# Two feed-forwards in split single precision: whole products in the first, seven block products kept for the second

## The chip, the core and the metric

The kernel runs on one core of a Trainium2 chip. The metric is device time in microseconds, as the median of several runs. TensorE (PE) does the matmuls, VectorE (DVE), ScalarE (ACT) and GpSimd (POOL) the element-wise work, SyncE (SP) issues the loads and stores.

## What is computed

Two batches of eight heads of attention over 768 positions: each query sees the keys within 16 positions and 24 block summaries (the maximum of 32 keys, the mean of 32 values). The result, 1,536 tokens of 512 numbers, goes through two feed-forwards.

```python
def _moe_ref(x, w_in, w_out):
    h = x @ w_in                      # 512 -> 2048
    g = h * np.cos(h)
    return (g @ w_out).astype(np.float32)

def _moe2_ref(x, w_in, w_out):
    h = x @ w_in
    relu6 = np.clip(h + 3.0, 0.0, 6.0)
    g = h * relu6 / 6.0
    return (g @ w_out).astype(np.float32)
```

The weights arrive in 64-bit floats.

## The kernel before

**Precision.** Every operand of a feed-forward matmul is split into a rounded part and its remainder (`whi`/`wlo`, `xhi`/`xlo`, `ghi`/`glo`), and a product is three matmuls: hi x hi, lo x hi, hi x lo.

**Steps.** The tokens are three blocks of 512 (`blk`), the hidden width is 16 slices of 128 (`f`) for each feed-forward (`m`). `plan` lists steps (m, blk, f, c0, c1) in groups of four slices; the blocks' direction turns with each group. A step is an input product (`mm1` or half of an `mm1_set`), the nonlinearity (`middle`, L796) and an output product (`mm2`, L853: 12 matmuls summed over the group's four slices in four banks of PSUM, then added to `total` by `close`, L893). The first 16 steps (`NEARLY`) work on halves of 256 tokens, as soon as the attention has delivered them; the next four are plain.

**Plain product** (`mm1`, L764): 12 matmuls of 512 columns into one bank; `middle` reads h from PSUM.

**Seven block products** (`mm1_set`, L708). From step `SETS` = 20 on, two slices of one block go together. The two slices and the two halves of the contraction form a 2 x 2 scheme: seven products of 256 columns, six matmuls each, instead of eight. That needs seven combined weight blocks for each pair of slices (`convert_pair`, L411, into `phi`/`plo`; two pairs are held), combined token blocks (`tees`, L673; `first_tees`, L702, rebuilds the first feed-forward's input as a sum first), and for every set two copies and five adds on 256 columns from PSUM into `hs` (L744 and the helper L389). `middle` then reads h from `hs`.

**Weights.** `nearest` (L431) loads a 64-bit slice into one of two `raw` buffers and rounds it to single precision in one of two pairs `cv_y`, `cv_t`: two conversions, a shift (L462), a merge (L464), an add (L466). `split` (L403) makes the rounded part (the helper `copy`, L389) and the remainder (L406). `convert` (L394) does this for a plain slice: six slots for output slices, four for input slices, which lie in the `phi` tiles.

**Nonlinearity.** In the first feed-forward: a rounding on ScalarE (L819), a subtraction (L821), the sine (L823), h times it (L825), then the rounded part (L389) and the remainder (L834). Three buffers for `c` (`ch_c`), four for `g`.

**Order.** All of this is recorded as operations with dependencies by keys. `Graph.run` gives each a due time and places them, with modelled costs, on the engines that may do them; the result is a fixed instruction order for each engine. Where the planner sees a gap before a matmul, `fill` (L839) puts matmuls on zeros (L844, L849) there. The output product of step s is recorded `LAG` = 2 steps behind its input product.

Of the kernel before, what the change touches and what calls it, by code (L numbers as in the profile page):

```python
# [11 lines left out]
F32 = mybir.dt.float32  # L12
# [17 lines left out]
LAG = 2  # L30
# [158 lines left out]
def attention_two_ffn(  # L189
# [47 lines left out]
    NPLAIN = GROUPS[0][0]  # L237
    SETS = NEARLY + NPLAIN

# [23 lines left out]
    def ring(p, name, n, shape, dtype=F32):  # L263
# [8 lines left out]
    per = -(-NPLAIN // NPAIR)  # L272
# [121 lines left out]
    def convert(n, side):  # L394
# [3 lines left out]
        i = slot(*slices[n]) if side == "out" else n  # L398
        y, _, yk, _ = nearest(n, side)
        new = ["room"] if NW0 <= n < NW1 else []  # L400
# [8 lines left out]
    def convert_pair(p):  # L409
# [250 lines left out]

    tx, hs = {"hi": [], "lo": []}, []
    NH = 4
    PAUSE = 0.3
# [7 lines left out]
    def tees(b, buf, bk):  # L671
# [29 lines left out]

    def first_tees(b):  # L702

        for kk in range(NK):
            G.op({"POOL": pool(TOK), "DVE": dve(TOK)}, lambda e, kk=kk: VEC[e].tensor_tensor(
                total[NBLK - 1][:, kk, :], xhi[b][:, kk, :].bitcast(F32), xlo[b][:, kk, :].bitcast(F32), ALU.add),
                r=["room"] + [(n, b, kk, o) for n in ("xh", "xl") for o in range(UPB)],
                w=[("total", NBLK - 1, kk)], twice=True)  # L708
        tees(b, lambda: total[NBLK - 1], ("total", NBLK - 1))
# [78 lines left out]
    def ring_of(s):  # L788

        if s < NEARLY:  # L790
            return s % NC, s % NG

        return s % NC1, (3, 1, 0, 2)[(s - NEARLY) % NG1]

    def middle(s):
        N = plan[s][4] - plan[s][3]  # L796
        i, n = ring_of(s)
        ck, gk = ("c", i), ("gh", n)
        room = ["room"] if i >= NC or n >= NG else []
# [11 lines left out]
        def c():  # L811
            return ch_c[i][:, 0:N]

        def gh():
            return ghi[n][:, 0:N]

        if plan[s][0] == 0:

            G.op({"ACT": act(N) + 0.05}, lambda e: nc.scalar.activation(  # L819
                c().bitcast(I32), h(), AF.Identity, bias=quarter, scale=0.5 / math.pi), r=hk + room, w=[ck])  # L820
# [247 lines left out]
```

## Time and profile before

| | us |
|---|---|
| median of 3 runs (614.90 to 615.78) | 615.45 |
| profiled execution, its own time | 615.68 |
| its span, first to last instruction | 614.0 |
| TensorE busy | 592.5 |
| VectorE busy | 515.4 |
| ScalarE busy | 389.2 |
| GpSimd busy | 230.4 |

Busy time is the sum over instructions, idle time is what lies between them. A line such as "idle before, releaser" says what ended the idle time. The granted clock is a share of 2.4 GHz.

### The profile page before, as it was taken

How to read it: one execution, taken by the hardware profiler on the slowest of the kernel's cores; microseconds unless marked ns; L12 is line 12 of the kernel's file. 1: busy time of each engine (PE TensorE's matmuls, PEld its weight loads, DVE VectorE, ACT ScalarE, POOL GpSimd, SP SyncE). 2: the span in 40 equal slices, each digit the busy share in tenths (PEclk: the TensorE clock that was granted, in tenths of full speed). 3: DMA queues.
4: the chain of work that ended last, by engine and by line, in shares of the span. 5: the costliest groups of instructions: out<-in, count | busy, mean ns of one | idle time of the engine just before them, and what ended most of it. 6: DMA issues, size and time to landing. Idle time of an engine off the chain costs nothing.

```text
span 614.0 us, 11095 instructions
## 1 busy us (share of the span) xinstructions
PE 592.5 (97%) x4244; PEld 519.5 (85%) x4244; DVE 515.4 (84%) x916; ACT 389.2 (63%) x828; POOL 230.4 (38%) x216
## 2 busy tenths in 40 slices
PE   9989899998998999999989999999999999999997
PEld 6678698887897888988978888999898989889895
DVE  4889997699999999899999999989869984984644
ACT  4889997675667667657776675685845643462321
POOL 5245531444232743473455554434334311520110
PEclk9999999999999999999999999999999999999999
DMA  8768631012112222111212012122312320200111
GB/s 275 226 233 254 183 122 52 2 69 69 34 36 69 69 69 69 70 68 70 76 62 70 25 46 69 49 90 98 108 69 70 114 92 1 70 1 1 69 70 68
DMA packets 17141, 51.57 MB, mean 84 GB/s; under 512 B 2112, under 2 KB 2112, under 8 KB 17088
## 3 DMA queue, kind: packets, MB, share of 16 engines
q1 hardware_dynamic: 17088, 50.86, 25.2%
q8 instruction: 33, 0.54, 0.4%
q14 instruction: 20, 0.16, 0.1%
HBM read 47.71 MB, written 3.15 MB: 83 GB/s over the span
## 4 chain that ended last, share of the span: by engine, by line
PE 55%; DVE 17%; ACT 6%; issue 3%; POOL 2%; DVEq 0%; ACTq 0%; POOLq 0%
PE bank_a L874 15%; PE bank_d L731 12%; PE bank_b L874 7%; PE bank_c L874 7%; PE bank_e L731 6%; PE bank_c L731 6%; DVE ch_c L821 2%; DVE hs L744 2%; DVE glo L834 1%; DVE ch_c L825 1%; DVE cv_t L464 1%; DVE ch_c L830 1%; ACT ch_c L823 1%; POOL cv_y L466 1%; ACT ch_c L819 1%
## 5 line engine op out<-in xcount | busy, mean ns | idle before, releaser
L466 POOL TENSOR_TENSOR cv_y<-cv_t,cv_y 128x512 int32<-128x512 int32 x29 | 42.4, 1463 | 75.9 <-DVE cv_t L464 64.8
L744 DVE TENSOR_TENSOR hs<-bank_d,hs 128x256 f32<-128x256 f32 x108 | 45.1, 421 | 29.3 <-PE bank_d L731 27.2
L834 POOL TENSOR_TENSOR glo<-ch_c,ghi 128x512 fp32r<-128x512 f32 (+1 forms) x28 | 34.2, 1227 | 52.5 <-ACT ghi L389 47.2
L389 ACT CAST ghi<-ch_c 128x512 fp32r<-128x512 f32 (+1 forms) x74 | 43.5, 592 | 11.6 <-DVE ch_c L825 5.4
L828 ACT ACTIVATE ch_c<-hs,three 128x512 f32<-128x512 f32 x48 | 33.7, 722 | 26.8 <-DVE hs L744 26.3
L464 DVE SCALAR_TENSOR_TENSOR cv_t<-raw,cv_t 128x512 int32<-128x512 int32 x64 | 49.2, 780 | 0.2
L457 ACT ACTIVATE cv_t<-raw 128x512 f32<-128x512 f32 x59 | 39.3, 670 | 6.2 <-DMA raw<-in_w_out_dram 2.3
L823 ACT ACTIVATE ch_c<-ch_c,half_pi 128x512 f32<-128x512 f32 (+1 forms) x56 | 35.8, 659 | 8.4 <-DVE ch_c L821 8.3
L830 DVE SCALAR_TENSOR_TENSOR ch_c<-ch_c,hs 128x512 f32<-128x512 f32 x48 | 36.9, 778 | 4.1 <-ACT ch_c L828 2.6
L447 ACT ACTIVATE cv_y<-raw 128x512 int32<-128x512 uint32 x54 | 35.8, 671 | 4.4 <-DVE wlj_out L406 3.5
L834 DVE TENSOR_TENSOR glo<-ch_c,ghi 128x512 fp32r<-128x512 f32 (+1 forms) x54 | 37.0, 692 | 1.7 <-POOL ghi L389 0.7
L731 PE MATMUL bank_d<-xhi,phi 128*128 128x256 f32 x170 | 34.7, 286 | 3.3 <-DVE hs L744 2.4
L731 PEld LDWEIGHTS bank_d<-xhi,phi 128*128 128x128 f32 x170 | 28.4, 189 | 8.3 <-DVE hs L744 3.9
L834 POOL TENSOR_TENSOR glj<-ch_c,ghj 128x512 fp32r<-128x512 f32 x11 | 15.9, 1443 | 51.5 <-ACT ghj L389 48.4
L462 DVE TENSOR_SCALAR cv_t<-cv_t 128x512 int32<-128x512 int32 x64 | 32.5, 516 | 2.3 <-ACT cv_t L457 2.2
L731 PE MATMUL bank_d<-xlo,phi 128*128 128x256 f32 x170 | 34.2, 283 | 0.0
L406 POOL TENSOR_TENSOR plo<-cv_y,phi 128x512 fp32r<-128x512 f32 (+1 forms) x16 | 18.6, 1161 | 41.6 <-DVE phi L389 33.8
L731 PE MATMUL bank_d<-xhi,plo 128*128 128x256 f32 x170 | 34.2, 282 | 0.0
L819 ACT ACTIVATE ch_c<-hs,quarter 128x512 int32<-128x512 f32 x36 | 24.9, 720 | 13.2 <-DVE hs L744 13.1
L821 DVE SCALAR_TENSOR_TENSOR ch_c<-hs,ch_c 128x512 f32<-128x512 f32 x36 | 31.2, 889 | 0.8 <-ACT ch_c L819 0.5
L825 POOL TENSOR_TENSOR ch_c<-hs,ch_c 128x512 f32<-128x512 f32 x14 | 20.7, 1486 | 29.5 <-ACT ch_c L823 29.5
L389 ACT COPY hs<-bank_d 128x256 f32<-128x256 f32 x39 | 14.5, 372 | 26.9 <-PE bank_d L731 26.5
(359 smaller groups left out, 2023.5 us busy)
## 6 DMA issues: line engine op xcount, KB each, us to landing
raw<-in_w_in_dram SPq DMA_DIRECT2D x32, 512.0 KB, 3.5
raw<-in_w_out_dram SPq DMA_DIRECT2D x32, 512.0 KB, 3.4
vcat<-in_vw_dram SPq DMA_DIRECT2D x12, 384.0 KB, 4.3
ktile<-in_kt_dram SPq DMA_DIRECT2D x8, 384.0 KB, 4.4
qt<-in_q_dram SPq DMA_DIRECT2D x12, 256.0 KB, 5.4
total<-in_vw_dram SPq DMA_DIRECT2D x16, 128.0 KB, 3.9
out_dram<-total SPq DMA_DIRECT2D x8, 256.0 KB, 2.0
vnat<-in_vw_dram SPq DMA_DIRECT2D x8, 128.0 KB, 5.8
```

The costliest lines, as they stand in the source:

```text
L389: nc.scalar.copy(o, i) if e == "ACT" else VEC[e].tensor_copy(o, i)
L447: nc.scalar.activation(y, low.bitcast(U32), AF.Copy, scale=2.0 ** -29)
L457: nc.scalar.activation(o, a, AF.Copy, scale=2.0 ** -112)
L464: G.op({"DVE": dve(DM)}, lambda e: nc.vector.scalar_tensor_tensor(t, high, -0x80000000, t, ALU.bitwise_and, ALU.bitwise_or), r=[rk], w=[tk ...
L466: G.op({"POOL": pool(DM), "DVE": dve(DM)}, lambda e: VEC[e].tensor_tensor(y, t, y, ALU.add), r=[tk], w=[yk], twice=True)
L731: nc.tensor.matmul(o, wt[i][:, A[a], kk * P:(kk + 1) * P], xt[:, kk, :], start=first and n + kk == 0, stop=n + kk == 3, skip_group_check=True)
L744: G.op({"DVE": dve(HALF)}, lambda e: nc.vector.tensor_tensor(o[0](), a, b[0](), ALU.add), r=[ak, b[1], "room"], w=[o[1]])
L821: G.op({"DVE": dve(N)}, lambda e: nc.vector.scalar_tensor_tensor(c(), h(), 0.5 / math.pi, c().bitcast(I32), ALU.mult, ALU.subtract), r=hk, ...
L823: G.op({"ACT": act(N) + 0.1}, lambda e: nc.scalar.activation(c(), c(), AF.Sin, bias=half_pi, scale=2.0 * math.pi), w=[ck], table="sin")
L830: G.op({"DVE": dve(N)}, lambda e: nc.vector.scalar_tensor_tensor(c(), c(), 6.0, h(), ALU.min, ALU.mult), r=hk, w=[ck], twice=bool(both))
L834: G.op({"DVE": dve(N), "POOL": pool(N)}, lambda e: VEC[e].tensor_tensor(glo[n][:, 0:N], c(), gh().bitcast(F32), ALU.subtract), r=[ck, gk], ...
L874: nc.tensor.matmul(acc(s, i)[0], l, r, start=first, stop=end and p == 2 and (N == TOK or i % 2 == 1), skip_group_check=N < TOK)
```

## The change

The first feed-forward takes plain products for all its steps: `SETS` becomes the first step of the second feed-forward (56), and `first_tees` goes. The `phi` tiles hold six input slices then (`PER` = 3 in each of two), as many as the output slots; a freed slot takes the slice six ahead. Pairs are formed for the second feed-forward alone: the first two when the last reader of the three slots in their tile is done. Between step 16 and `SETS`, `c` and `g` have five buffers each: two `hs` buffers serve as `c`, and one token block of the `tees` of block 0, not yet needed, as `g` (`LENT`). There the output product follows three steps behind (`LAG1`). The order of first products, nonlinearities and output products is written as a list `events`, from which `assign` gives each step its `g` buffer.

```diff
-LAG = 2
+LAG, LAG1 = 2, 3
...
-    NPLAIN = GROUPS[0][0]
-    SETS = NEARLY + NPLAIN
+    SETS = next(s for s in range(NSTEP) if plan[s][0])
...
-    NW0, NW1 = NPLAIN, 6
+    NW0, NW1 = 4, 6
     NPAIR = 2
+    PER = 3
...
-        t[f // per][:, f % per * 2:f % per * 2 + 2, :].rearrange("p a c -> p (a c)") for f in range(NPLAIN)]}
+        t[f // PER][:, f % PER * 2:f % PER * 2 + 2, :].rearrange("p a c -> p (a c)") for f in range(PER * NPAIR)]}
...
-    NC, NC1 = 3, 3
+    NC, NCL = 3, 5
     ch_c = ring(main, "ch_c", NC, [P, TOK])
-    NG, NG1 = LAG + 1, 4
+    NG, NG1, NGL = 3, 4, 5
...
-        i = slot(*slices[n]) if side == "out" else n
+        i = slot(*slices[n]) if side == "out" else n % (PER * NPAIR)
...
-            also = [(n, "in", f) for n in ("whi", "wlo") for f in range(NPLAIN) if f // per == i] if p < per + NPAIR else []
+            also = [(n, "in", PER * i + f) for n in ("whi", "wlo") for f in range(PER)] if p < NF // 2 + NPAIR else []
...
+    LENT = (0, 0)
...
+                if (b, t) == LENT:
+                    hk, lk = hk + [("gh", NG1)], lk + [("gl", NG1)]
...
-    def first_tees(b):
...
-    def ring_of(s):
-
-        if s < NEARLY:
-            return s % NC, s % NG
-
-        return s % NC1, (3, 1, 0, 2)[(s - NEARLY) % NG1]
+    gslot = {}
+
+    def assign():
...
+    def gbuf(part, n):
+        if n == NG1:
+            return tx[part][LENT[0]][:, LENT[1]].rearrange("p a c -> p (a c)")
+        return {"hi": ghi, "lo": glo}[part][n]
+
+    def cbuf(s):
+
+        i = s % (NCL if NEARLY <= s < SETS else NC)
+        return (ch_c[i], ("c", i)) if i < NC else (hs[i - NC], None)
...
-    for n in range(NW0):
+    for n in range(PER * NPAIR):
         for side in SIDES:
             convert(n, side)
-    for n in range(NW0, NW1):
-        convert(n, "out")
...
     pending = []
     for s in range(NSTEP):
+        if s < SETS:
+            events += [("first", s), ("middle", s)]
+        elif (s - SETS) % 2 == 0:
+            while len(pending) > 2:
+                events.append(("second", pending.pop(0)))
+            events += [("set", s), ("middle", s), ("middle", s + 1)]
+        events.append(("used", s))
+        pending.append(s)
+        lag = LAG if s < NEARLY else (LAG1 if s < SETS else 2)
+        while pending and pending[0] <= s - lag and (s < SETS or (s - SETS) % 2):
+            events.append(("second", pending.pop(0)))
+    events += [("second", r) for r in pending]
+    assign()
...
-        if s == SETS:
-            for c in dict.fromkeys(x[1] for x in plan[s:s + NPLAIN * NBLK]):
-                first_tees(c)
...
+        elif s == uses[m, f]:
+            now = s
+            if n < NF - PER * NPAIR:
+                convert(n + PER * NPAIR, "in")
+            elif n < NF:
+
+                gone.add(n % (PER * NPAIR))
+                for i in range(NPAIR):
+                    if gone >= set(range(PER * i, PER * i + PER)):
+                        gone -= set(range(PER * i, PER * i + PER))
+                        convert_pair(NF // 2 + i)
+            elif n % 2:
+                convert_pair(n // 2 + NPAIR)
```

What it moves stands in the engines' lists. The first place is TensorE behind the four plain steps of block 2, where slices 4 and 5 begin. In the lists L731 is the set's line before and L726 after, L775 the plain product's line after, L874 and L896 the output product's. Before, the first set:

```order
L731 MATMUL bank_d0_107<-xhi2_96,phi0_69 128x256 x2
L731 MATMUL bank_d0_107<-xhi2_96,plo0_71 128x256 x2
L731 MATMUL bank_d0_107<-xlo2_99,phi0_69 128x256 x2
L731 MATMUL bank_d1_108<-txhi2_1611,phi0_69 128x256 x2
L731 MATMUL bank_d1_108<-txhi2_1611,plo0_71 128x256 x2
L731 MATMUL bank_d1_108<-txlo2_1614,phi0_69 128x256 x2
```

After, at the same place: the product of slice 3, the last of the four, then the output product of slice 0, and inside its end the product of slice 4, which is plain now:

```order
L775 MATMUL bank_c1_106<-xhi2_96,phi1_70 128x512 x4
L775 MATMUL bank_c1_106<-xhi2_96,plo1_72 128x512 x4
L775 MATMUL bank_c1_106<-xlo2_99,phi1_70 128x512 x4
L896 MATMUL bank_a0_102<-txhi0_1665,whi_out0_73 128x512
L896 MATMUL bank_a0_102<-txhi0_1665,wlo_out0_77 128x512
L896 MATMUL bank_a0_102<-txlo0_1668,whi_out0_73 128x512
...
L775 MATMUL bank_d0_107<-xhi2_96,phi1_70 128x512 x2
L896 MATMUL bank_c0_105<-txhi0_1665,whi_out0_73 128x512
```

Slice 4's products of 256 columns became products of 512 that need neither the token blocks `tx` nor adds; `txhi0` here is the lent buffer with g in it.

The second place is ScalarE in the last attention units, with the exponentials of the softmax (L600, after L599), the sine (L823, after L845) and the first feed-forward's rounding (L819, after L841). Before:

```order
L600 ACT_TABLE_LOAD
L600 ACTIVATE es_122,sm_132<-bank_c_105,nmx_130 128x120 x4
L600 ACTIVATE es_122,sm_132<-bank_c_106,nmx_130 128x120 x4
L389 COPY total_100<-bank_a_103 128x2x256
L819 ACTIVATE ch_c_85<-bank_d_108,quarter 128x256
L389 COPY pts_126<-bank_b 120x512
L819 ACTIVATE ch_c_86<-bank_d_107,quarter 128x256
L600 ACTIVATE es_123,sm_131<-bank_c_105,nmx_129 128x120 x4
L600 ACTIVATE es_123,sm_131<-bank_c_106,nmx_129 128x120 x4
L389 CAST xhi_96<-bank_e 128x4x128
L823 ACT_TABLE_LOAD
```

After:

```order
L599 ACT_TABLE_LOAD
L599 ACTIVATE es_122,sm_132<-bank_c_105,nmx_130 128x120 x4
L599 ACTIVATE es_122,sm_132<-bank_c_106,nmx_130 128x120 x4
L841 ACTIVATE ch_c_86<-bank_d_107,quarter 128x256
L845 ACT_TABLE_LOAD
L845 ACTIVATE ch_c_85<-ch_c_85,half_pi 128x256
L845 ACTIVATE ch_c_86<-ch_c_86,half_pi 128x256
L446 ACTIVATE cv_y_81<-raw_67 128x512
L388 COPY pts_126<-bank_b 120x512
L388 CAST ghi_88<-ch_c_85 128x256
L599 ACT_TABLE_LOAD
L599 ACTIVATE es_123,sm_131<-bank_c_105,nmx_129 128x120 x4
```

Two softmaxes (units in `es_122` and `es_123`) that shared one table now have the sine between them: two table loads more in the whole list, 16 where there were 14.

The third place is TensorE at the handover from the first feed-forward to the second, in the list of the change: the last reads of `phi0` as a plain slice, and the first set on pair 8 in the same tile.

```order
L775 MATMUL bank_e_109<-xhi0_94,phi0_69 128x512 x2
L775 MATMUL bank_e_109<-xhi0_94,plo0_71 128x512 x4
L775 MATMUL bank_e_109<-xlo0_97,phi0_69 128x512 x4
L896 MATMUL bank_a0_102<-txhi0_1665,whi_out3_76 128x512
...
L896 MATMUL bank_c0_105<-glo1_92,whi_out1_74 128x512
L726 MATMUL bank_d0_107<-xhi2_96,phi0_69 128x256 x2
L726 MATMUL bank_d0_107<-xhi2_96,plo0_71 128x256 x2
L726 MATMUL bank_d0_107<-xlo2_99,phi0_69 128x256 x2
L726 MATMUL bank_d1_108<-txhi2_1667,phi0_69 128x256 x2
```

Between the last read and the first set stand 48 matmuls of 512 columns, 36 of output products and 12 of slice 15. Before, a whole set of pair 7 (42 of 256) and 46 of output products stood there.

## Rows read from the trace of the kernel before

**Rows 1.** The page, busy us, share of the span and instructions.

```profile
PE 592.5 (97%) x4244; PEld 519.5 (85%) x4244; DVE 515.4 (84%) x916; ACT 389.2 (63%) x828; POOL 230.4 (38%) x216
```

**Rows 2.** Stretches: us, PE, PEld, DVE, ACT, POOL busy, granted clock, DMA, GB/s.

```profile
124.00:144.12 20.12, 19.85 (x101) 16.77 (x100) 18.99 (x32) 15.05 (x29) 6.39 (x7) 1.00 0.19 68
144.00:154.00 10.00, 8.15 (x52) 7.30 (x51) 9.88 (x16) 4.58 (x9) 5.81 (x4) 0.88 0.32 91
144.12:360.78 216.66, 208.78 (x1283) 186.22 (x1282) 203.19 (x348) 145.45 (x265) 99.60 (x73) 0.99 0.19 62
360.78:609.60 248.82, 246.85 (x1520) 220.81 (x1518) 194.85 (x349) 128.63 (x234) 74.52 (x60) 1.00 0.18 61
```

**Rows 3.** The same from 144.12 us, for L731, L874 and L849 alone.

```profile
144.12:360.78 216.66, 107.37 (x822) 104.01 (x821) 0.99 0.19 62
144.12:360.78 216.66, 111.75 (x457) 84.29 (x457) 0.99 0.19 62
144.12:360.78 216.66, 1.42 (x4) 0.69 (x4) 0.99 0.19 62
```

**Rows 4.** TensorE's waits, 144 to 361 us: us in total, times, longest.

```profile
PE bank_d L731 <- DVE hs L744: 4.3, 5, 1.9
PE bank_e L731 <- DVE hs L744: 2.2, 4, 1.0
PE bank_d L731 <- ACT hs L389: 0.7, 1, 0.7
```

**Rows 5.** Timeline of TensorE, 354 to 361 us: start, us, instruction.

```profile
354.28 0.39 PE L874 MATMUL bank_a<-ghi,whi_out 128*128 128x512 f32 x1
...
357.91 0.40 PE L731 MATMUL bank_d<-xhi,phi 128*128 128x256 f32 x2
...
360.54 0.40 PE L731 MATMUL bank_d<-xlo,phi 128*128 128x256 f32 x2
360.78 0.40 PE L874 MATMUL bank_a<-whj_out,ghj 128*128 128x512 f32 x1
```

**Rows 6.** The same, a plain product, 129 to 132 us.

```profile
129.03 1.09 PE L780 MATMUL bank_d<-xhi,phi 128*128 128x512 f32 x4
...
131.78 0.28 PE L874 MATMUL bank_a<-ghi,whi_out 128*128 128x256 f32 x1
```

**Rows 7.** The same, 148 to 154 us.

```profile
148.41 0.40 PE L874 MATMUL bank_c<-ghi,whi_out 128*128 128x512 f32 x1
150.66 0.51 PE L731 MATMUL bank_d<-xhi,phi 128*128 128x256 f32 x2 [1.85 <-DVE hs L744]
...
153.53 0.63 PE L874 MATMUL bank_b<-ghi,wlo_out 128*128 128x512 f32 x1
153.96 0.63 PE L874 MATMUL bank_c<-ghi,wlo_out 128*128 128x512 f32 x1
```

**Rows 8.** The page's groups: count, busy us, mean ns, idle before.

```profile
L466 POOL TENSOR_TENSOR cv_y<-cv_t,cv_y 128x512 int32<-128x512 int32 x29 | 42.4, 1463 | 75.9 <-DVE cv_t L464 64.8
L744 DVE TENSOR_TENSOR hs<-bank_d,hs 128x256 f32<-128x256 f32 x108 | 45.1, 421 | 29.3 <-PE bank_d L731 27.2
L464 DVE SCALAR_TENSOR_TENSOR cv_t<-raw,cv_t 128x512 int32<-128x512 int32 x64 | 49.2, 780 | 0.2
L462 DVE TENSOR_SCALAR cv_t<-cv_t 128x512 int32<-128x512 int32 x64 | 32.5, 516 | 2.3 <-ACT cv_t L457 2.2
L406 DVE TENSOR_TENSOR plo<-cv_t,phi 128x512 fp32r<-128x512 f32 x23 | 16.8, 729 | 2.1 <-ACT phi L389 1.9
```

**Rows 9.** Timeline of ScalarE, 111 to 113 us.

```profile
111.56 1.28 ACT L823 ACT_TABLE_LOAD   x1
112.86 0.91 ACT L823 ACTIVATE ch_c<-ch_c,half_pi 128x256 f32<-128x256 f32 x2
```

**Rows 10.** Timeline of TensorE, 379 us.

```profile
379.03 0.74 PE L874 MATMUL bank_a<-whi_out,glo 128*128 128x512 f32 x2 [1.26 <-DVE glo L834]
```

**Rows 11.** TensorE's waits, 84 to 124 us.

```profile
PE bank_d L780 <- DVE ch_c L825: 1.3, 2, 0.9
```

More of the change, by code (lines that the diff above doesn't have):

```diff
@@ L397, in convert @@
             return
-        i = slot(*slices[n]) if side == "out" else n
+        i = slot(*slices[n]) if side == "out" else n % (PER * NPAIR)
         y, _, yk, _ = nearest(n, side)
-        new = ["room"] if NW0 <= n < NW1 else []
+        new = ["room"] if NW0 <= n < NW1 and side == "out" else []
         split(lambda: whi[side][i], lambda: wlo[side][i], y.bitcast(F32), [yk] + new, ("whi", side, i), ("wlo", side, i), DM)
@@ L700, in tees @@
         parts(0, b22, down)
-    def first_tees(b):
[L704 to L709, printed above, removed]
     def mm1_set(s, due):
@@ L786, in mm1 @@
                 ], w=[hk], due=due + (2 * p + k0 // 2) * 2 * mm(n))
-    def ring_of(s):
-        if s < NEARLY:
-            return s % NC, s % NG
-        return s % NC1, (3, 1, 0, 2)[(s - NEARLY) % NG1]
+    gslot = {}
+    def assign():
+        free, kept = list(range(NG)), []
+        for what, s in events:
+            if what == "second":
+                kept.append(gslot[s])
+            elif what == "middle":
+                n = NG if s < NEARLY else (NGL if s < SETS else NG1)
+                free += kept
+                kept = []
+                for k in range(n):
+                    if k not in free and k not in [gslot[r] for r in gslot if r not in done]:
+                        free.insert(0, k)
+                gslot[s] = next(k for k in free if k < n)
+                free.remove(gslot[s])
+            if what == "second":
+                done.add(s)
+    done, events = set(), []
+    def gbuf(part, n):
[5 more added lines that the diff above has]
+        return (ch_c[i], ("c", i)) if i < NC else (hs[i - NC], None)
     def middle(s):
         N = plan[s][4] - plan[s][3]
-        i, n = ring_of(s)
-        ck, gk = ("c", i), ("gh", n)
-        room = ["room"] if i >= NC or n >= NG else []
+        n = gslot[s]
+        late_c = NEARLY <= s < SETS and s % NCL >= NC
+        ck = [("h", s % NCL - NC, t) for t in range(2)] if late_c else [cbuf(s)[1]]
+        gk = ("gh", n)
+        room = ["room"] if late_c or n >= NG else []
         if s < SETS:
@@ L856, in mm2 @@
         begin, end = opens[s], closes[s]
-        wi, n = slot(m, f), ring_of(s)[1]
-        parts = (("whi", whi, "gh", ghi), ("wlo", wlo, "gh", ghi), ("whi", whi, "gl", glo))
+        wi, n = slot(m, f), gslot[s]
+        parts = (("whi", whi, "gh", "hi"), ("wlo", wlo, "gh", "hi"), ("whi", whi, "gl", "lo"))
         order = [[(p, i) for i in (i0, i0 + 1)] for p in range(3) for i0 in (0, 2)]
@@ L866, in go @@
                 for p, i in group:
-                    l, r = parts[p][1]["out"][wi], parts[p][3][n][:, 0:N]
+                    l, r = parts[p][1]["out"][wi], gbuf(parts[p][3], n)[:, 0:N]
                     if m == 0:
@@ L967, in switch @@
         wlo["out"] += ring(pool, "wlj_out", NW1 - NW0, [P, DM], F32R)
-        ch_c.extend(ring(pool, "ch_d", NC1 - NC, [P, TOK]))
         ghi.extend(ring(pool, "ghj", NG1 - NG, [P, TOK], F32R))
@@ L990, in second @@
             convert(slices.index((m, f)) + NW1, "out")
+    gone = set()
     pending = []
     for s in range(NSTEP):
+        if s < SETS:
[11 more added lines that the diff above has]
+    assign()
+    now = 0
+    for what, s in events:
         m, b, f, _, _ = plan[s]
         n = slices.index((m, f))
-        if s == SETS:
-            for c in dict.fromkeys(x[1] for x in plan[s:s + NPLAIN * NBLK]):
-                first_tees(c)
-        if s < SETS:
+        if what == "first":
+            now = s
             mm1(s, when(s))
+        elif what == "set":
+            now = s
+            mm1_set(s, when(s))
+        elif what == "middle":
             middle(s)
-        elif (s - SETS) % 2 == 0:
-            mm1_set(s, when(s))
-            middle(s)
-            middle(s + 1)
-        if s == uses[m, f] and n % 2:
-            convert_pair((n + 1) // 2 - 1 + NPAIR)
-        pending.append(s)
-        while pending and pending[0] <= s - LAG and (s < SETS or (s - SETS) % 2):
-            second(pending.pop(0), when(s) + 2.6)
-    for r in pending:
-        second(r, when(NSTEP) + 2.6)
+        elif what == "second":
+            second(s, when(now) + 2.6)
+        elif s == uses[m, f]:
+            now = s
+            if n < NF - PER * NPAIR:
[8 more added lines that the diff above has]
+                convert_pair(n // 2 + NPAIR)
+        else:
+            now = s
     with tc.manual_schedule():
```

21 lines of the change are left out of this document (10 added, 11 removed).

## The prediction

> **What bounds the kernel now.** I read the page first: TensorE is busy for 592.5 of 614.0 us and VectorE for 515.4 [rows 1]. So close to full, the question is not which engine bounds but how much of TensorE's time is neither work nor needed. The stretches answer it. From 144.12 us, where the first seven-product set starts, to 360.78 us, where the second feed-forward's first output product starts, lie 216.66 us, in which VectorE is busy for 203.19, that is 94% [rows 2]. In the same stretch stand 822 matmuls of 256 columns (L731), 456 of 512 (L874; the 457th starts at its end) and 4 filler matmuls of 512 columns on zeros (L849) [rows 3].
>
> What they need undisturbed comes from the timeline: 24 matmuls of 256 columns from 357.91 to 360.78 us, 0.1196 us each, and 16 of 512 columns from 354.28 to 357.91, 0.2269 us each [rows 5]. So 822 x 0.1196 + 456 x 0.2269 = 98.3 + 103.5 = 201.8 us of work in 216.66 us: **14.9 us are lost**, 0.9 of it in fillers. The list of TensorE's waits says to whom: nearly all stand before a product (L731) and end with a VectorE add into hs (L744), the longest 1.9 us [rows 4]. After that one the clock falls as well: TensorE starts again at 150.66, the matmuls from 153.53 on come 0.43 us apart instead of 0.227 [rows 7], and the mean granted clock of 144 to 154 us is 0.88 [rows 2], which is the 1.2 GHz level for a part of it. The last stretch, from 360.78 to 609.60, takes 248.82 us for 942 and 576 matmuls, which need 243.4: 5.4 us lost, with VectorE at 78% [rows 2]. VectorE is late where it is fullest, and there TensorE waits.
>
> **The change, part by part.** (1) *Whole products.* 18 sets of 42 matmuls of 256 columns (5.02 us) become 36 steps of 12 matmuls of 512 (24 per pair, 5.45 us): 0.42 us more per pair, 7.6 us in all. The plain steps of the kernel before show 12 of 512 columns in 2.75 us, 0.229 each [rows 6], which gives 8.6. I take 7.8, nearer to the 16 in a row, since most matmuls will stand in such rows. The output products are the same number on both sides.
>
> The Trainium skill ("TensorE: Matmul & The Clock Gate", section on the back-to-back issue gap) gives 262 cycles for 256 columns and 518 for 512, by which two narrow matmuls cost hardly more than a wide one. By its figures the cost would be 10.7 us and the sum 2.9 us higher, an estimate from that page. The trace differs: 0.1196 and 0.2269 us are 287 and 545 cycles at 2.4 GHz, so I give that sum 1 in 100, inside the case "within" below.
>
> (2) *What VectorE and ScalarE lose.* 18 sets x 5 adds of 0.42 us [rows 8] are 38 us off VectorE; the 36 copies of a product into hs, mostly ScalarE's, go with them, and so do the first set of block sums and differences (first_tees and its tees) and the half-slice sums of six pairs. On VectorE's list of the change I count 253 rows from the first 512-wide step to the first add of the second feed-forward; at some 0.56 us each (0.6 for 512 columns, 0.34 for 256) they are about 142 us in some 215, 66% where it was 94%. c and gh now read the product from PSUM, but in five buffers and three steps behind, so a late VectorE no longer stops the next product.
>
> (3) *The 14.9 us.* With the adds gone their waits go, and the fillers: the change's list has no filler behind the attention. What can come back is bounded by zero and by the only plain steps of before, 124.00 to 144.12 us, where TensorE is idle for 0.27 in 20 us [rows 2], 2.7 us over 197. I take 1.0, because that stretch still had VectorE at 94%.
>
> (4) *The handover.* Pair 8 (slices 16, 17) now needs slots 0 to 2 of the first feed-forward free. Between the last read of phi0 and the first product of pair 8 the list has 48 matmuls of 512 columns, 10.9 us; before it was 46 of 512 and 42 of 256, 15.5 us. Queued behind it are pair 9 (the cv buffers are two) and the output slices that use the same two. The cover is a third shorter, so I charge a stall: between zero and the 2.0 us lost at 148.41 plus 1.7 for the clock behind it [rows 7], taking 1.5 after the one stall at the second feed-forward's opening, 1.26 us plus its restart [rows 10].
>
> (5) *Up to 124 us.* The planner shuffles the last attention units: 8 filler matmuls of 256 columns where there were 2, and two more table loads on ScalarE, of 1.28 us each [rows 9]. Idle time of ScalarE can take these. From below: the 1.3 us that TensorE waited for ch_c there [rows 11] may vanish. From above: 2 x 1.28 + 6 x 0.12 = 3.3 us. I take the fillers alone, 0.7.
>
> (6) *No price*: raw loads are the same 64 of 512 KB; the six slots are rings in tiles that exist already; LENT gives g a buffer whose own first use lies behind the handover. The cover is 5.45 us of TensorE work per step; if a buffer came late it would show as a wait before an output product, and I have priced that in (3). The last stretch keeps its 5.4 us, give or take 1.5.
>
> The sum against the profiled execution: 614.0 - 14.9 + 7.8 + 1.0 + 1.5 + 0.7 = 610.1 us of span. Its own time was 615.68, 1.68 outside the span, so 611.8; the median of the runs, 615.45, lies 0.23 lower: **611.6 us**.
>
> **Rivals.** *Deeper.* Handover and attention both stay hidden and VectorE's slack carries into the second feed-forward: without (4) and (5), and 0.9 off the last stretch, 608.5 us. For it: the planner put no filler at the handover. Against: stalls of 0.2 to 1.3 us are in every part of the trace [rows 4, 10].
>
> *The attention pays, and nothing is won.* There ScalarE has the softmax and the sine in turn, one table each; if both added loads lie on the chain, (5) costs 3.3 instead of 0.7: 614.2 us, and with a stall more at the handover 614.9: within 0.2% of before. For: the units are in one chain through ScalarE. Against: the load at 111.56 us shows ScalarE going on 0.02 us after it, at 112.86 [rows 9], so 1.28 us is all that one costs. The Trainium skill ("ScalarE: Activation LUTs", section on what a table load costs) counts another 1.38 us of drain for each switch, by which two would be 5.3 us and the sum 616.2; no row of this trace shows such a drain.
>
> *Slower: the handover breaks.* Pair 9 waits for the cv buffers of pair 8. A pair is two shifts (0.52), two merges (0.78), two sums (1.46 on POOL), four half sums (0.42, by L744) and four remainders (0.73) [rows 8], 10.1 us. If neither were begun before phi0 is free, VectorE would have 14.3 us of them (POOL the two sums of each) and about 29 rows of its own between, of some 0.6 us each, 17.4 us: 31.7 us, where TensorE has 21.3 us of work up to pair 9's first product (72 matmuls of 512 columns, 42 of 256). 10.4 us late, 1.7 for the clock, in place of my 1.5: 622.2 us. It decides the sign from 6.6 us of lateness on. Against: only the last writes wait for phi0; the shifts and merges stand ahead of it in VectorE's list.
>
> *It doesn't do what it says.* If sets stayed in the first feed-forward, the time would stay too. The list has 1,008 matmuls on the set's line where it had 1,764, which leaves little room.
>
> **How the numbers follow.** The forecast, 609.5 to 613.8 us, gets 0.60; deeper 0.18; the attention's price 0.11; no real change and the page's pitch 0.03 together; the broken handover 0.08. What a measurement of this kernel can tell from no change is about 0.2%, 1.2 us: 614.2 to 616.7 is "within". Faster is 0.78, within 0.14, slower 0.08. The range, 607.8 to 614.8, takes in the deeper case and the attention's bound and leaves out the broken handover, a few of the best sums and of the worst.
>
> **What would show it.** Right: matmuls of 512 columns at 0.227 us from about 140 us on, up to 36 x 5.45 us later; TensorE's waits there below 2 us in sum; VectorE at 65 to 72% there; no fall of the granted clock after 130 us; the second feed-forward's opening product waiting for phi for under 2 us. Wrong: a gap of several us before the first set of pair 8 or 9, waits behind table loads before 124 us, or a pitch near 0.235 for the wide matmuls.

## The result and the profile after

| | before | after |
|---|---|---|
| median, us (4 runs each on one chip) | 615.17 (614.38 to 615.78) | 609.69 (608.78 to 610.08) |
| ratio, 95% interval | | 0.9909 (0.9892 to 0.9927) |
| profiled execution, its own time | 615.68 | 609.72 |
| its span | 614.0 | 608.0 |

Faster by 5.5 us, 0.9%. The forecast was 611.6 with a range of 607.8 to 614.8.

The page of the changed kernel, the line that answers to [rows 1]:

```profile
PE 593.8 (98%) x3922; PEld 508.7 (84%) x3922; DVE 463.2 (76%) x825; ACT 359.3 (59%) x745; POOL 162.1 (27%) x170
```

TensorE is busy 1.3 us longer and the span is 6.0 us shorter. VectorE is busy for 52 us less and GpSimd for 68. The stretches of the changed kernel answer to [rows 2] (us, PE, PEld, DVE, ACT, POOL busy, granted clock, DMA, GB/s). They are cut at the first set (340.11), behind the first two sets (356.81) and where [rows 2] lets the second feed-forward run on:

```profile
125.00:144.12 19.12, 19.12 (x98) 16.28 (x97) 15.87 (x26) 13.54 (x23) 8.11 (x7) 1.00 0.35 110
144.12:340.11 195.99, 195.99 (x867) 162.28 (x865) 141.20 (x232) 102.74 (x163) 28.49 (x25) 1.00 0.17 54
340.11:356.81 16.70, 14.83 (x98) 13.27 (x96) 15.74 (x24) 9.10 (x20) 9.64 (x8) 1.00 0.18 62
356.81:394.00 37.19, 36.35 (x226) 32.52 (x225) 34.04 (x60) 25.55 (x50) 14.70 (x11) 1.00 0.21 70
394.00:603.76 209.76, 209.06 (x1289) 187.42 (x1288) 156.34 (x290) 103.18 (x187) 46.77 (x37) 1.00 0.17 60
```

From 125.00 to 340.11 us TensorE is busy in every microsecond, at full granted clock, with VectorE at 72 to 83%. What is left stands behind 340.11. TensorE's waits from 340 us to the end (us in total, times, longest), to set against [rows 4]:

```profile
PE bank_c L726 <- ACT hs L388: 2.0, 2, 1.8
PE bank_d L726 <- DVE hs L739: 1.1, 2, 0.8
PE bank_e L726 <- DVE hs L739: 0.2, 1, 0.2
```

From 117 to 340 us the same view has one line, a wait of 0.6 us before 124 us. On TensorE's timeline four wide matmuls start every 0.91 us, 0.227 each:

```profile
125.00 1.09 PE L775 MATMUL bank_d<-xhi,phi 128*128 128x512 f32 x4
125.93 1.07 PE L775 MATMUL bank_d<-xhi,plo 128*128 128x512 f32 x4
126.84 1.07 PE L775 MATMUL bank_d<-xlo,phi 128*128 128x512 f32 x4
127.75 1.07 PE L775 MATMUL bank_d<-xhi,phi 128*128 128x512 f32 x4
```

Three of the page's groups answer to [rows 8] (count, busy us, mean ns, idle before):

```profile
L463 DVE SCALAR_TENSOR_TENSOR cv_t<-raw,cv_t 128x512 int32<-128x512 int32 x64 | 44.7, 704 | 0.3
L739 DVE TENSOR_TENSOR hs<-bank_d,hs 128x256 f32<-128x256 f32 x60 | 25.2, 422 | 20.0 <-PE bank_d L726 18.3
L461 DVE TENSOR_SCALAR cv_t<-cv_t 128x512 int32<-128x512 int32 x64 | 31.4, 493 | 1.5 <-ACT cv_t L456 1.5
```

The adds into hs (L739, L744 before) are fewer at the same 0.42 us. The merges (L463, L464 before) are the same 64 instructions, and each takes 704 ns on average where it took 780: the first trace of what follows.

I settle the account as the prediction did: **lost time** is the distance between two starts on TensorE's timeline less 0.1196 us for each matmul of 256 columns and 0.2269 for each of 512, with fillers counted as work. Before, 14.1 us are lost from 124.75 to 360.78, 1.9 from there to 395 and 3.6 behind that. After, it is -0.1 from 125.00 to 340.11, 2.6 in the first two sets, 1.3 up to 394 and 3.3 behind. So the 6.0 us of span are: stalls of the first feed-forward -14.3, fillers -0.9, columns +7.6, handover and opening of the second feed-forward +2.05 (2.64 + 1.30 against 1.88), the rest of it -0.3, the part up to 125 us +0.25, the tail behind the last matmul -0.4.

### The profile page after: what moved, and what is told of

Read it like the earlier page. It is cut to its first block, busy times and chain, and to the rows that moved or that the text cites. A ratio compares the mean times of both kernels' runs of the same rounds, so it can differ in the third digit from the quotient of the medians.

```text
span 608.0 us, 10176 instructions
## 1 busy us (share of the span) xinstructions
PE 593.8 (98%) x3922; PEld 508.7 (84%) x3922; DVE 463.2 (76%) x825; ACT 359.3 (59%) x745; POOL 162.1 (27%) x170
## 4 chain that ended last, share of the span: by engine, by line
PE 80%; DVE 9%; ACT 7%; DMA 2%; issue 1%; SPq 0%; POOL 0%; ACTq 0%; POOLq 0%; DVEq 0%
PE bank_a L896 20%; PE bank_d L775 11%; PE bank_b L896 9%; PE bank_c L896 9%; PE bank_d L726 9%; PE bank_e L726 5%; PE bank_e L775 4%; PE bank_c L726 4%; PE bank_c L775 4%; ACT es L599 2%; DVE total L934 1%; DVE ch_c L852 1%; DMA raw<-in_w_in_dram 1%; PE bank_c L569 1%; PE bank_e L516 1%
## 5 line engine op out<-in xcount | busy, mean ns | idle before, releaser
L463 DVE SCALAR_TENSOR_TENSOR cv_t<-raw,cv_t 128x512 int32<-128x512 int32 x64 | 44.7, 704 | 0.3
L739 DVE TENSOR_TENSOR hs<-bank_d,hs 128x256 f32<-128x256 f32 x60 | 25.2, 422 | 20.0 <-PE bank_d L726 18.3
L775 PE MATMUL bank_d<-xhi,phi 128*128 128x512 f32 (+1 forms) x144 | 36.9, 352 | 1.7 <-DVE ch_c L847 1.6
L845 ACT ACTIVATE ch_c<-ch_c,half_pi 128x512 f32<-128x512 f32 (+1 forms) x40 | 25.3, 637 | 14.1 <-DVE ch_c L843 14.0
L775 PE MATMUL bank_d<-xhi,plo 128*128 128x512 f32 (+1 forms) x144 | 32.3, 344 | 0.0
L775 PE MATMUL bank_d<-xlo,phi 128*128 128x512 f32 (+1 forms) x144 | 32.2, 344 | 0.0
L775 PEld LDWEIGHTS bank_d<-xhi,phi 128*128 128x128 f32 x144 | 23.9, 188 | 8.3 <-DVE ch_c L847 3.2
L599 ACT ACTIVATE es<-bank_c,nmx 128x120 f32<-128x120 f32 x88 | 30.4, 374 | 0.6 <-DVE nmx L591 0.5
L465 DVE CUSTOM_DVE_ANT_0 cv_y<-cv_t,cv_y 128x1024 uint16<-128x1024 uint16 x41 | 29.1, 717 | 2.2 <-ACT cv_y L446 1.5
L775 PEld LDWEIGHTS bank_d<-xhi,plo 128*128 128x128 f32 x144 | 23.9, 189 | 3.4 <-issue 0.2
L775 PEld LDWEIGHTS bank_d<-xlo,phi 128*128 128x128 f32 x144 | 23.9, 189 | 3.3
L841 ACT ACTIVATE ch_c<-bank_d,quarter 128x256 int32<-128x256 f32 (+1 forms) x28 | 16.0, 573 | 17.8 <-PE bank_d L775 17.7
L896 PE MATMUL bank_a<-ghi,whi_out 128*128 128x256 f32 (+1 forms) x92 | 24.3, 324 | 0.7 <-POOL ghi L388 0.7
```

Source lines behind the costliest of these rows:

```text
L463: G.op({"DVE": dve(DM)}, lambda e: nc.vector.scalar_tensor_tensor(t, high, -0x80000000, t, ALU.bitwise_and, ALU.bitwise_or), r=[rk], w=[tk ...
L465: G.op({"POOL": pool(DM), "DVE": dve(DM)}, lambda e: VEC[e].tensor_tensor(y, t, y, ALU.add), r=[tk], w=[yk], twice=True)
L599: nc.scalar.activation(ef[:, c, :], s4[j][:, hp, :], AF.Exp, bias=nmx[:, c:c + 1], scale=scale, accum_out=sm[:, c:c + 1])
L775: nc.tensor.matmul(h, w["in"][i][:, kk * P:(kk + 1) * P], x[blk][:, kk, c0:c1], start=p + kk == 0, stop=p == 2 and kk == NK - 1)
L896: nc.tensor.matmul(acc(s, i)[0], l, r, start=first, stop=end and p == 2 and (N == TOK or i % 2 == 1), skip_group_check=N < TOK)
```

## The experiments

The stalls went when the sets went. The prediction said why: VectorE was full there, so its adds came late. Four theories stood against each other:

- **A**, VectorE's load makes the adds late.
- **B**, the order inside a set (product, add, next product in the same bank) waits whatever VectorE does.
- **C**, the five buffers and the longer lag hide it.
- **D**, added after the runs e1, e2, e4 and e7: GpSimd makes single VectorE instructions long, and a set's add stands in line behind one.

"Before" in each ratio is the kernel before, run on the same chip; medians of different runs are often from different chips.

### The depth: e1_shallow

```diff
-LAG, LAG1 = 2, 3
+LAG, LAG1 = 2, 2
-    NC, NCL = 3, 5
+    NC, NCL = 3, 3
-    NG, NG1, NGL = 3, 4, 5
+    NG, NG1, NGL = 3, 4, 4
```

> The changed kernel with the depth of before in the first feed-forward: three c buffers, four g buffers, products two steps behind, everything else as changed. Theory A (VectorE's load made the adds late) and theory B (a set waits inside itself for adds and copies of its own banks, a whole product does not): the whole products need no depth, TensorE still has no wait between 125 and 340 us, time within 1 us of the changed kernel (609.7). Theory C (the five buffers and the third step of lag are what hides the waits): some us of waits come back on the products of the second layer, 613 us or more.

612.03 us (610.69 to 612.32), ratio 0.995 (0.9936 to 0.9965). Lost time up to the first set: -0.2 us. So whole products need no depth in the first feed-forward, and **C falls**. The median is 2.3 us above that of the changed kernel all the same, more than the 1 us that A and B allowed. The profiled execution, the fastest of the four and 1.0 us above the changed kernel's in span, loses 3.9, 2.3 and 4.0 us in the three stretches behind the first set in place of 2.6, 1.3 and 3.3: the handover has another order there. What makes up the rest of the 2.3 us isn't shown.

### VectorE's load: e2_dve_load, e2b_dve_half, e4_before_relieved

The changed kernel with VectorE filled up:

```diff
             middle(s)
+            if NEARLY <= s < SETS:
+                h, hk = hbank(s)
+                for _ in range(4):
+                    G.op({"DVE": 0.0}, lambda e, h=h, b=b: nc.vector.tensor_tensor(
+                        hs[3][:, 0:HALF], h[:, 0:HALF], xhi[b][:, 0, 0:HALF].bitcast(F32), ALU.add),
+                        r=[hk, "room"], w=[("h", 3, 0)])
```

> The changed kernel with four adds of 256 columns more in each of the 36 plain steps of 512 columns of the first feed-forward (144 adds, they read the step's own bank and write a buffer that nobody reads), which brings VectorE there from about 66% to about 94% busy, its load in the kernel before. Theory A (the load alone made the waits): the waits of before come back, some 10 to 14 us, 620 us or more. Theory B (the waits belong to the set's own order of product, add and next product in the same bank): 609.7 to 612 us, TensorE still with under 2 us of waits between 144 and 340 us.

636.74 us, ratio 1.0351 (1.0334 to 1.0368). TensorE's waits in the plain steps of this run, 144 to 362 us:

```profile
PE bank_a L896 <- DVE total L934: 6.5, 2, 6.3
PE bank_a L896 <- DVE totak L934: 4.4, 1, 4.4
PE bank_a L896 <- ACT totak L928: 3.0, 1, 3.0
```

These are not the waits of before: no input product waits, but the first output product of a block, for the sums that close the block before it. VectorE was asked for more than the time there was: 141.2 us of its own in 196 us, and 144 adds of 0.42 us make some 202, where 94% was meant. That is 6 us too much, and over 20 are lost, while VectorE is 87% busy:

```profile
144.12:362.00 217.88, 202.91 (x866) 165.18 (x865) 188.54 (x364) 99.68 (x163) 33.83 (x31) 0.97 0.15 51
```

A backlog that grows within a block and is waited for at its end would fit; no run took this apart. The time is the one that A named, the waits are not. With two adds in place of four:

> The changed kernel with two adds of 256 columns more in each of the 36 plain steps (72 instead of 144 as in the run before, 30 us of VectorE), VectorE at about 83% in the first feed-forward. If VectorE's load costs time step by step, about half of what 144 adds cost: 620 us or more. If it costs only where a backlog builds up that the slack between bursts can't clear, little or nothing: 612 us or less.

609.57 us (608.34 to 611.49), ratio 0.9899 (0.9871 to 0.9927): the time of the changed kernel. VectorE's row for the plain steps of this run:

```profile
144.12:340.28 196.16, 196.16 (x867) 162.34 (x866) 164.22 (x299) 101.37 (x166) 30.15 (x28) 1.00 0.16 57
```

84% busy, and TensorE has no idle time. Between 84% and more than there is stands no run: whole products at the 94% of before were not tried.

The other side: the kernel before, with work taken off VectorE.

```diff
+        skip = m == 0 and f >= 4
-        G.op({"DVE": dve(DM, 2)}, lambda e: nc.vector.tensor_scalar(
+        G.op({"DVE": dve(DM, 2)}, lambda e: None if skip else nc.vector.tensor_scalar(
...
-        G.op({"DVE": dve(DM)}, lambda e: nc.vector.scalar_tensor_tensor(
+        G.op({"DVE": dve(DM)}, lambda e: None if skip else nc.vector.scalar_tensor_tensor(
```

> The kernel before, with two VectorE operations left out of each weight conversion of the first feed-forward's slices 4 to 15 (the shift and the merge of the exponent: 48 instructions, some 32 us of VectorE; these slices' weights are then other numbers), the order of all other instructions as in the kernel before. VectorE falls from 94% to about 79% busy between 144 and 361 us. Theory A: most of the 14 us of lost time there goes, 605 us or less. Theory B: it stays, 612 us or more.

612.88 us (612.5 to 613.24), ratio 0.9964 (0.9953 to 0.9976), as B had it and A did not. Its row for the stretch of the sets:

```profile
144.12:360.78 216.66, 209.68 (x1289) 187.25 (x1288) 184.77 (x314) 147.51 (x269) 95.71 (x72) 0.99 0.17 59
```

And VectorE's timeline at one of the stalls (start, us, instruction):

```profile
183.51 1.78 DVE L695 TENSOR_TENSOR totak<-totak 128x512 f32<-128x512 f32 x1
185.22 0.41 DVE L745 TENSOR_TENSOR hs<-bank_e,hs 128x256 f32<-128x256 f32 x1
```

VectorE fell from 203.2 to 184.8 us of 216.66 and the lost time only from 14.0 to 12.5, with the stalls at the same places. The same stall in the kernel before, on the timeline of all engines:

```profile
184.23 1.36 POOL L825 TENSOR_TENSOR ch_c<-hs,ch_c 128x512 f32<-128x512 f32 x1 [2.16 <-ACT ch_c L823]
...
184.35 1.79 DVE L694 TENSOR_TENSOR totak<-totak 128x512 f32<-128x512 f32 x1
...
186.06 0.41 DVE L744 TENSOR_TENSOR hs<-bank_e,hs 128x256 f32<-128x256 f32 x1
...
186.53 0.50 PE L731 MATMUL bank_e<-xhi,phi 128*128 128x256 f32 x2 [0.85 <-DVE hs L744]
```

An addition of 512 columns (L694) takes 1.79 us, and 0.68 where nothing runs beside it. GpSimd started 0.12 us earlier; VectorE's instruction ends 0.55 us after GpSimd's. The set's add (L744) stands in VectorE's queue behind it, and TensorE waits. The long stall of [rows 7] looks the same: L466 took 1.78 and L449 1.48 us ahead of the add.

```profile
146.79 1.53 POOL L834 TENSOR_TENSOR glo<-ch_c,ghi 128x512 fp32r<-128x512 f32 x1 [0.18 <-ACT ghi L389]
...
147.09 1.78 DVE L466 CUSTOM_DVE_ANT_0 cv_y<-cv_t,cv_y 128x1024 uint16<-128x1024 uint16 x1
...
148.28 1.71 POOL L705 TENSOR_TENSOR totak<-xhi,xlo 128x512 f32<-128x512 f32 x1
...
148.79 1.48 DVE L449 TENSOR_SCALAR cv_y<-raw 128x512 int32<-128x512 uint32 x1
150.19 0.41 DVE L744 TENSOR_TENSOR hs<-bank_d,hs 128x256 f32<-128x256 f32 x1
```

That is theory D. Of the nine waits of [rows 4] that end with an add, seven have such a stretched instruction, of 0.95 to 1.8 us, among the last four ahead of the add. The other two, at 190.16 and 283.15 us, have only a row of instructions of ordinary length there.

### GpSimd left out of the kernel before: e8_before_no_pool

```diff
+        if self.leave and "POOL" in engines:
+            keep, e0 = self.keep, fn
+            fn = lambda e: (keep and keep()) if e == "POOL" else e0(e)
```

`leave` holds from the first set to the end of the first feed-forward; `keep` is ScalarE's copy.

> The kernel before, with the 70 GpSimd instructions of the first feed-forward's sets left out (from the first set on; where one writes a buffer for the first time ScalarE copies something into it instead, 21 copies), VectorE's own instructions and the order of everything else as before; left out are additions, remainders and products, so the numbers are others. Theory D (a VectorE instruction beside a running GpSimd instruction takes 1.5 to 1.8 us instead of 0.4 to 0.7, and a set's add stands in line behind it): the lost time between the first set and the end of the first feed-forward falls from 14.0 us to under 6, 607 us or less. Theory B (the set's own order of product, add, next product is enough by itself): it stays above 11 us, 612 us or more.

604.32 us (604.13 to 604.8), ratio 0.9822 (0.9801 to 0.9842). The same stretch:

```profile
144.12:360.78 216.66, 214.82 (x1343) 193.30 (x1343) 186.58 (x364) 157.61 (x293) 12.61 (x10) 1.00 0.18 61
```

Lost time 4.1 us in place of 14.0. VectorE's share, 86%, is that of e4 (85%), where 12.5 were lost: at the same load GpSimd makes the difference, so **A falls as the cause, and B keeps at most the 4 us**. The run also takes away every wait for a result of GpSimd's, which is a rival; but VectorE's list of waits in this stretch of the kernel before has only two for GpSimd, of 0.6 and 0.4 us, and TensorE's has none. One and the same instruction, the subtraction behind the rounding, in the stretch's groups by line (count, busy us, mean ns), before:

```profile
L821 DVE SCALAR_TENSOR_TENSOR ch_c<-hs,ch_c 128x512 f32<-128x512 f32 x36 | 31.2, 889 | 0.8 <-ACT ch_c L819 0.5
```

And in this run:

```profile
L833 DVE SCALAR_TENSOR_TENSOR ch_c<-hs,ch_c 128x512 f32<-128x512 f32 x36 | 24.1, 685 | 2.3 <-ACT ch_c L831 1.9
```

889 ns on average became 685. The adds into hs, with one operand in PSUM, took 420 ns in both. The run leaves work out, so it prices GpSimd's presence and is no version.

### GpSimd kept out, nothing left out: h1, h2, g1, g2

```diff
+        if self.alone and "DVE" in engines:
+            engines = {k: v for k, v in engines.items() if k != "POOL"}
```

An operation that may run on VectorE no longer may on GpSimd, and the planner orders everything anew. `alone` holds for a stretch of steps in each run. In the changed kernel, around the handover:

> The changed kernel with no shared operation given to GpSimd around the handover (from 12 steps before the first set to 4 steps behind it: what could run on either goes to VectorE). Theory D: VectorE's instructions there no longer stretch, and of the 3.9 us lost between 340 and 394 us two or more go: 606 to 608 us. If VectorE is simply full there, the stalls grow: 610 us or more. Theory B: unchanged, 609 to 610 us.

606.78 us (606.72 to 607.21), ratio 0.9862 (0.9842 to 0.9882). Lost in the first two sets: 0.1 us in place of 2.6; a stall of 1.6 us came in at 373 us, beyond the edge of the edit. To the end of the program:

> The changed kernel with no shared operation given to GpSimd from 12 steps before the first set to the end. Theory D: of the 7.2 us lost behind 340 us four or more go, 604 to 606 us, though VectorE rises from 76% to some 85% busy in the second feed-forward. If VectorE's load is what counts: 611 us or more. Theory B: 609 to 610 us.

602.67 us (602.26 to 603.54), ratio 0.9795 (0.9774 to 0.9817), better than expected: of the 7.2 us lost behind 340 us, 1.2 stay. The stretches of this run from the plain steps on:

```profile
144.12:339.31 195.19, 195.19 (x863) 161.60 (x861) 144.08 (x246) 102.76 (x163) 10.09 (x8) 1.00 0.16 54
339.31:356.00 16.69, 16.69 (x114) 15.40 (x112) 16.69 (x35) 11.15 (x23) 0.00 (x0) 1.00 0.19 64
356.00:394.00 38.00, 38.00 (x238) 34.30 (x237) 37.57 (x75) 25.54 (x49) 0.00 (x0) 1.00 0.21 72
394.00:596.95 202.95, 202.95 (x1262) 183.33 (x1261) 160.39 (x326) 97.70 (x176) 0.00 (x0) 1.00 0.17 61
```

TensorE's list of waits is empty behind 124 us, and that with VectorE busy 16.69 us of 16.69 at the handover and 99% in the stretch behind it. 47 us of GpSimd's in the last stretch cost VectorE only 4 us more than in the last stretch of the changed kernel, since its other instructions got shorter: counting what each takes beyond the shortest of its line and form, some 14 us became 3.

The same edit in the kernel before, from the first set on:

> The kernel before with no shared operation given to GpSimd from the first set on to the end: all of them stay in the program and go to VectorE. With 70 GpSimd instructions left out altogether, VectorE was busy 186 of 216 us there (86%); moving them to VectorE instead, at some 0.6 us each, makes that 228 of 216 us. Theory D with VectorE full: the sets of the first feed-forward become bound by VectorE, 615 us or more, some 10 us or more in the first feed-forward lost, while the second loses under 1 us. If the kernel before only had a wrong division of work between the two engines: 604 us or less, and the change to whole products was not needed.

603.95 us (602.98 to 604.6), ratio 0.982 (0.9798 to 0.9843). **I expected 615 or more; this is the miss that teaches most.** It meets the other branch, 604 us or less, by which the kernel before had a wrong division of work and whole products were not needed. Its stretch of sets:

```profile
144.12:360.78 216.66, 214.45 (x1323) 191.69 (x1322) 214.93 (x427) 148.92 (x270) 3.54 (x3) 1.00 0.17 62
```

VectorE is at 99%, more than in the kernel before (94%), and 6.5 us are lost where 14.0 were. I had charged 70 instructions of 0.6 us on top of e8's 186 us; this run has 63 more than e8 in the stretch and 28 us more, 0.45 each. No VectorE instruction in this stretch takes 0.7 us or more beyond the shortest of its kind, so hardly any of what is still lost is D. From 12 steps before the second feed-forward on:

> The kernel before with no shared operation given to GpSimd from 12 steps before the second feed-forward to the end (what was done to the changed kernel in the run that came to 602.7). Theory D: the 1.9 and 3.6 us lost behind 361 us go, and some of what is lost in the last 12 steps before: 609 to 611 us, so that the gain of the change and that of this edit add up. If VectorE is too full at the end of the sets of the first feed-forward: 613 us or more.

609.6 us (609.51 to 609.87), ratio 0.9912 (0.9896 to 0.9928), the time as expected, though only half of the 5.4 us lost behind 361 us goes (2.6 stay), and the sets lose 3.1 us less. The stretch of sets side by side, by lost time; "stretched" counts the VectorE instructions in it that take 0.7 us or more beyond the shortest of the same line and form:

| kernel | VectorE, us of 216.66 | GpSimd | stretched | lost, us |
|---|---|---|---|---|
| before | 203.2 | 99.6 | 19 | 14.0 |
| before, 48 VectorE instructions left out (e4) | 184.8 | 95.7 | 18 | 12.5 |
| before, GpSimd off for the last part (g2) | 206.2 | 67.2 | 11 | 10.9 |
| before, GpSimd off (g1) | 214.9 | 3.5 | 0 | 6.5 |
| before, GpSimd's work left out (e8) | 186.6 | 12.6 | 2 | 4.1 |

The lost time follows GpSimd's column and the stretched instructions, not VectorE's, save between the last two rows, where VectorE's 99% may tell. The window is the same in all rows, so a faster kernel has more of the second feed-forward in it; over the 18 sets alone the losses are 13.9, 12.5, 9.9, 5.8 and 4.1 us, in the same order.

### Whole products in both feed-forwards: e7_whole_both

```diff
-    SETS = next(s for s in range(NSTEP) if plan[s][0])
+    SETS = NSTEP
...
-        n = TOK if i >= NK // 2 else HALF
+        n = TOK
...
-            if i == NK - 1:
-                tees(blk, lambda: total[blk], ("total", blk))
...
-            if n < NF - PER * NPAIR:
+            if n < len(slices):
```

> Whole products in both feed-forwards: the changed kernel with the 24 sets of the second feed-forward as 48 whole products too, no slices' sums and no token sums. Columns: 24 sets at 0.42 us each cost 10.1 us more. Waits: the changed kernel loses 2.6 + 1.3 + 3.3 = 7.2 us after 340 us; by theories A and B nearly all of that goes, which gives 609.7 + 10.1 - 7 = 612.8 us (range 611 to 615). If a handover between the two feed-forwards costs some us whatever the form of the products, 615 or more; below 609.7, and the sets do not pay in the second feed-forward either.

611.5 us (611.12 to 613.38), ratio 0.9952 (0.9934 to 0.997). Lost behind 125 us: -0.4, that is nothing. But the conditions changed too: without the token and slice sums GpSimd works for 13 us behind 340 us, where the changed kernel has 71, and VectorE is 53% busy there. That a whole product, with no add inside, is less open to this wait shows better in e1: between 144 and 340 us GpSimd works for 40 us, three VectorE instructions are stretched by 0.7 us or more, and TensorE doesn't wait. Whole products beside the 99.6 us of GpSimd's work of before were not run. In the span 10.1 us of columns came in and 7.5 of lost time went; the sets of the second feed-forward pay 1.9 us as the changed kernel has them, and 8.8 us (611.5 against 602.7, on two chips) with GpSimd off.

### The two best side by side: h2_again, g1_again

> The changed kernel without shared operations on GpSimd from 12 steps before the first set on, once more, on one chip with the next one, to tell whether whole products in the first feed-forward are worth anything once GpSimd stands still: by the two spans (601.2 and 601.7 us) it is 0.5 us ahead of the next one, less than can be told; by the first medians (602.7 and 604.0) 1.3 us.

> The kernel before without shared operations on GpSimd from the first set on, on one chip with the one above: 603 to 604 us. If it is level with the one above, the 7.6 us of columns that whole products cost equal what VectorE at 99% loses in the sets; if it is 1 us or more behind, whole products still pay a little.

603.24 us, ratio 0.9806 (0.9786 to 0.9825), and 604.66 us, ratio 0.9831 (0.9814 to 0.9849). The changed kernel with GpSimd off is ahead by 1.4 us here and by 1.3 in the first pair, which was on two chips. The intervals of the ratios overlap, but on the one chip all runs of the one (601.47 to 603.72) lie below all of the other (603.94 to 605.26): a small gain is likely, by which whole products still pay a little. **Both beat the changed kernel by 5 to 7 us.**

## Why the prediction was right, and where it was not

The sign, the range and most sizes held; the reason given for the largest term did not.

**What bounds the kernel.** "VectorE is late where it is fullest, and there TensorE waits": the second half held, the first is the step that failed. The waits were indeed for VectorE's adds [rows 4], but not because it was 94% busy. e4 with 85% keeps most of them, g1 with 99% is rid of more than half, and e2b puts 84% on whole products at no cost. What made seven of the nine adds late was an instruction ahead of them, stretched beside GpSimd, at the worst from 0.4 or 0.7 to 1.5 or 1.8 us; the other two may be load or the sets' own order. The rows to see it in stood in the trace of before: L466 at 1.78 us and L449 at 1.48 ahead of the late add of [rows 7], and groups of the same shape with means between 0.68 and 0.89. No term of the prediction looked at what GpSimd does to VectorE. The 14.9 us went all the same, since by A, B and D alike the waits go with the sets: that the largest term came out is no support for the reason given, and in that respect luck.

The Trainium skill ("SBUF — State Buffer", section on SBUF's two separate sides) says that VectorE and GpSimd share one pair of ports as an exclusive lock: a VectorE instruction with two SBUF inputs, beside a GpSimd instruction that reads SBUF and started first, is blocked until the other ends. The trace agrees: L694 reads two SBUF tensors and ends 0.55 us after GpSimd's instruction, and L744, with one input in PSUM, keeps its 0.42 us. I had not used it. In this trace instructions with one SBUF input are stretched as well: L449 and L462 take 0.42 us alone and up to 1.48 and 1.52 beside GpSimd.

**(1) Columns**, 7.8: 7.6 measured, with the wide matmuls at 0.227 us from 125 us on. The sum 2.9 us higher, by the Trainium skill ("TensorE: Matmul & The Clock Gate", section on the back-to-back issue gap), did not come.

**(2) VectorE's share**, 66%: from 125.00 to 340.11 us it was 157.1 of 215.1 us, 73%. I counted 253 rows and took 0.56 us each; there were 258 of 0.61, since some still met GpSimd: about 10 us are what single instructions took beyond the shortest of their kind. The five buffers and the three steps, which the term relied on as well, were not needed (e1).

**(3) What comes back**, 1.0: nothing came back. The bound of zero was the value; the argument for 1.0, VectorE's load in the plain steps of before, is the one that fell.

**(4) The handover**, 1.5: 3.9 us in the two stretches behind 340 us, against 1.9 in that part before; together with (6) it is 7.2 against 6.9 forecast. The place was right, and the mechanism resembled that of the broken handover, at a third of its size: pair 9 was prepared late (the 14.3 us of that sum add up to 14.4). But no product waited for phi, neither at the opening nor behind it; what came late was a copy. The timeline of the changed kernel there, GpSimd and VectorE:

```profile
346.92 1.47 POOL L698 TENSOR_TENSOR total<-total 128x512 f32<-128x512 f32 x1
...
347.16 1.50 DVE L405 TENSOR_TENSOR plo<-cv_y,phi 128x256 fp32r<-128x256 f32 x1
...
348.46 1.35 POOL L680 TENSOR_TENSOR total<-total 128x512 f32<-128x512 f32 x1
...
348.59 1.50 DVE L422 TENSOR_TENSOR cv_t<-cv_t,cv_y 128x256 f32<-128x256 f32 x1
```

Two instructions of 0.42 us take 1.50 each beside GpSimd's work on the token sums. ScalarE then waits for L422, and its queue runs late (its own timeline):

```profile
350.13 0.62 ACT L388 CAST phi<-cv_t 128x512 fp32r<-128x512 f32 x1 [3.88 <-DVE cv_t L422]
...
354.31 0.66 ACT L456 ACTIVATE cv_t<-raw 128x512 f32<-128x512 f32 x1
354.88 0.35 ACT L388 COPY hs<-bank_c 128x256 f32<-128x256 f32 x1
```

The copy out of bank_c, whose product TensorE had finished three microseconds earlier, is the tenth instruction from 350.13 on; TensorE waits for it:

```profile
355.28 0.50 PE L726 MATMUL bank_c<-xhi,phi 128*128 128x256 f32 x2 [1.82 <-ACT hs L388]
```

The run h1 removes the overlap, and the loss in these two sets goes from 2.6 to 0.1 us. I had priced this preparation at VectorE's mean durations; the stretching was in none of the terms.

**(5) Up to 124 us**, 0.7: 0.25, the first wide product starting at 125.00 in place of 124.75. The two more table loads and the fillers together cost no more than that, and "the attention pays" falls.

**(6) The rest of the second feed-forward** lost 0.3 us less, not 0.9. *Deeper* named 608.5, nearer than my 611.6, but half of its mechanism, a hidden handover, was wrong. *It doesn't do what it says* falls with the list of waits.

The forecast lay 1.9 us above the median. In the span it was 2.1: 1.3 from (3) with the lost time, 0.45 from (5), 0.2 from (1), 0.7 from the tail and the rest, less 0.55 from (4).

**What the change did, then.** It paid 7.6 us of columns for 15.2. It took out the form of product that is open to a late VectorE, and with it most of the lateness: behind 144 us GpSimd works for 28.5 of 196 us where it was 99.6 of 217, and two VectorE instructions are stretched by 0.7 us or more where there were 19. The sums for the first feed-forward's sets are gone, and h times the sine, which GpSimd shared while h lay in `hs`, is VectorE's alone. Which of the two brought how much of the 15.2 us, no run tells. A cheaper cure was in the division of work between VectorE and GpSimd: g1 won 11.0 us, the change 5.5. What stays open: the 6.5 us that g1 still loses, with VectorE at 99% and nothing stretched, may be load or B; no run took them apart. A version with sets in a part of the first feed-forward and GpSimd off wasn't tried.

## What to carry to other kernels

A high busy share alone doesn't tell that an engine is late. Here most of the lateness came from instructions of unplanned length: compare each form's mean with its shortest, and look at what ran beside the long ones. Before you hand VectorE's work to GpSimd, count what it costs VectorE beside it; here 47 us on GpSimd were worth 4 on VectorE. When a change removes waits, test whether it removed their cause, what was exposed to it, or, as here, some of both.

## What was unexpected of the hardware

- VectorE with two SBUF inputs beside GpSimd: 0.41 to 0.42 us (256 columns) became up to 1.50, 0.68 (512 columns) up to 1.8. TENSOR_SCALAR with one SBUF input (512 columns): 0.42 up to 1.52. The adds with one input in PSUM (256 columns): 0.42 us with and without.
- A planned order held with VectorE busy in all of 16.69 us, and TensorE did not wait once.
- The granted clock was 0.92 from 144 to 166 us in the kernel before and 1.00 in every stretch of the changed one behind 125 us: with the stalls gone, the time at the lower level went too.
